# Linear attention and GeGLU on one core: denominators of all heads on column tiles, spread over the heads' rows by DMA

## The chip, the cores and the metric

The kernel runs on one core of a Trainium2 chip. The metric is the device time of one execution in microseconds (us), as the median of three runs. Five engines work side by side, each through its own instructions in order: PE (TensorE, matmuls; its weight loads are listed as PEld), DVE (VectorE), ACT (ScalarE), POOL (GpSimd) and SP (SyncE, which issues most of the DMA transfers). They wait for one another by semaphores.

## What is computed

A layer norm, a linear attention with 32 heads of 18 columns and a gated MLP, all on the same normalised input of 2048 tokens with 576 features, summed with the input:

```python
def _A_ref(x, wqkv, wo):                       # S = 2048, D = 576, H = 32, Dh = 18
    qkv = (x @ wqkv).reshape(B, S, 3, H, Dh).transpose(2, 0, 3, 1, 4)
    q, k, v = qkv[0], qkv[1], qkv[2]
    phi = lambda t: jnp.where(t > 0, t + 1, jnp.exp(t)) + 1e-6
    pq, pk = phi(q), phi(k)
    kv = jnp.einsum("bhsd,bhse->bhde", pk, v)
    z = jnp.einsum("bhsd->bhd", pk)
    num = jnp.einsum("bhqd,bhde->bhqe", pq, kv)
    den = jnp.einsum("bhqd,bhd->bhq", pq, z)[..., None] + 1e-6
    return (num / den).transpose(0, 2, 1, 3).reshape(B, S, D) @ wo

def _B_ref(x, w_gate, w_up, w_down):           # F = 4608
    return (_gelu(x @ w_gate) * (x @ w_up)) @ w_down

xn = _layernorm(x)
return x + _A_ref(xn, A_wqkv, A_wo) + _B_ref(xn, B_w_gate, B_w_up, B_w_down)
```

The denominator `den` is one number for each token and head. It divides 18 columns of the numerator, so it may as well divide the 18 rows of that head in the transposed `pq`.

## The kernel before

**Data.** `xnT` is the normalised input, transposed, features on the partitions. `pqT` is the transposed phi(q) in five chunks of heads: four of 7 heads (126 rows) and one of 4 heads (72 rows), each with 2048 tokens. Tokens are worked on in four groups of 512 (`sc` = 0 to 3). A unit of Q is one chunk of one group, 20 in all.

**Front** (to about 71 us). The layer norm, K, phi(K), the matrix G of phi(K) and the input, and most Q units run in an order written out by due times (`STEPS`, `Q_STEPS`, lines 530 to 583). What follows is written out as program order (lines 600 to 640): the rest of G, its copies to SBUF (`g_copy`), Q unit 12, the last rows of G (`g_last`), the column sums of phi(K) (`z_sums`, which uses four column tiles of 32), their copies (`z_copies`), Q unit 13, then `z_stage` and `kv_stage`. `z_stage` makes `zrep`: for each chunk a matrix in which every row of a head has that head's z, repeated for the head's 18 columns and masked elsewhere. A matmul with it gives the denominator already repeated over the head's rows. The last six Q units run as three pairs on row tiles (`q_pair`, `_Unit`): two units share the array, each on 64 of its rows, take nine slots instead of ten, and change places on the PSUM banks half way (`p1`, `p2`). For the change of places an empty instruction on another engine (the relay: SP for these pairs, POOL in the gate/up blocks after the first) waits for `p1` and releases `p2`.

**Gate/up stage** of each token group (`gu_pair`): 18 blocks of two units, each unit 18 row-tiled matmuls. ACT makes the gelu of one bank, DVE multiplies the other bank into `hT`. A block's weights (`wg`, `wu`, `wr`, four transfers) go to one of four buffers; they are issued on SP at the start of the block three earlier (`load_gu(blk + NWBUF - 1, i)`). In the first group, blocks 2 to 13 also issue one slice each of the down weights `wd_sb`.

**Denominators.** In the first group, blocks 2 to 4 carry three row-tiled pairs of denominator matmuls (`den_pair`, lines 498 and 687 to 699). The others (`den_mm`, line 495) run at the head of the half tiles of the down stage before. DVE copies each result to SBUF and adds the epsilon (`den_evac`), then inverts it in pieces of 128 columns (`den_norm`, line 519), and POOL multiplies `pqT` by it (line 522).

**Down stage** of each token group (`down_tile`): four tiles of 128 tokens in two halves of 288 columns; each half is 36 matmuls of `hT` with `wd_sb` (line 724) and 5 of `pqT` with `m_sb` (line 729). `m_sb` is made once from kv and wo (`m_stage`). DVE adds the input and SP writes the tile out. `hooks` lists what goes ahead of a half's matmuls.

Of the kernel before, what the change touches and what calls it, by code (L numbers as in the profile page):

```python
# [9 lines left out]
ALU = mybir.AluOpType  # L10
# [5 lines left out]
P = 128  # L16
HP = 64
# [22 lines left out]
TD = 4  # L40
XW = 640
PKW = 580


class _Ring:
# [11 lines left out]
def kernel(  # L57
# [68 lines left out]
    make_identity(nc, ident[:])  # L126
    eps_ln = const.tile([P, 1], F32, name="eps_ln")
    nc.vector.memset(eps_ln[:], EPS_LN)
    eps_att = const.tile([P, 1], F32, name="eps_att")
    nc.vector.memset(eps_att[:], EPS_ATT)  # L130

    def spin(count):

# [6 lines left out]
    pqT = persist.tile([P, NCH, S], BF16, name="pqT")  # L140
    wo2 = persist.tile([P, NCH, D], BF16, name="wo2")
    m_sb = persist.tile([P, NCH, D], BF16, name="m_sb")
    zrep = persist.tile([P, NCH, CR], BF16, name="zrep")
    kvT = persist.tile([P, NCH, CR], BF16, name="kvT")

    nc.vector.memset(pqT[HP:P, NCH - 1, 0:2 * SC], 0.0)
    nc.vector.memset(zrep[HP:P, NCH - 1, :], 0.0)

    def load_wo():
        nc.sync.dma_start(wo2[:CR, 0:4, :], A_wo[0:4 * CR, :].rearrange("(c p) j -> p c j", p=CR))  # L150
# [49 lines left out]
    nc.gpsimd.memset(g_sb[0:HP, 4, HALF:D], 0.0)  # L200
    nc.gpsimd.memset(g_sb[HP:P, 4, 0:HALF], 0.0)

    ZQ = 32
    z_ones = const.tile([P, ZQ], BF16, name="z_ones")
    nc.gpsimd.memset(z_ones[:], 1.0)
    z_sb = apool.tile([P, D], BF16, name="z_sb")
    nc.gpsimd.memset(z_sb[:], 0.0)
    zsel = const.tile([P, CR], BF16, name="zsel")
    nc.gpsimd.memset(zsel[:], 0.0)
    for g in range(P // ZQ):  # L210
        nc.gpsimd.memset(zsel[g * ZQ:g * ZQ + 1, :], 1.0)
# [109 lines left out]
    def z_sums(bank):  # L321
        for n in range(NS):
            for g in range(4):
                p0 = PK0[g // 2] + (g % 2) * DQ
                nc.tensor.matmul(
                    ps_all[g * ZQ:(g + 1) * ZQ, bank, 0:DQ], lhsT=z_ones[:], rhs=pk[:, n, p0:p0 + DQ],
                    start=(n == 0), stop=(n == NS - 1), skip_group_check=True,
                )
# [52 lines left out]
    def q_unit(i):  # L381
        sc, c = divmod(i, NCH)
        rows = DH * HCH[c]
        q0 = DH * HOFF[c]
        ps = ps_all[:rows, q_banks.next(), :]
        for kt in range(KT):
            nc.tensor.matmul(  # L387
                ps, lhsT=wqkv_sb[:, kt, q0:q0 + rows], rhs=xnT[:, kt, sc * SC:(sc + 1) * SC],
                start=(kt == 0), stop=(kt == KT - 1),
            )  # L390
        q_out[i] = ps
# [57 lines left out]
    def mask_pair(dst, b4, b1):  # L449

        nc.vector.tensor_tensor(
            out=dst[:CR, 0:4, :], in0=ps_all[:CR, b4, 0:4 * CR].rearrange("p (c d) -> p c d", c=4),
            in1=bmask[:CR, :].unsqueeze(1).to_broadcast([CR, 4, CR]), op=ALU.mult,
        )
        r4 = DH * HCH[4]
        nc.vector.tensor_tensor(
            out=dst[:r4, 4, :r4], in0=ps_all[:r4, b1, 0:r4], in1=bmask[:r4, :r4], op=ALU.mult,
        )

    def chunk_out(c, b4, b1):  # L460
        rows = DH * HCH[c]
        return ps_all[:rows, b4, c * CR:c * CR + rows] if c < 4 else ps_all[:rows, b1, 0:rows]

    def z_stage(b4, b1):
        for c in range(NCH):
            rows = DH * HCH[c]
            nc.tensor.matmul(
                chunk_out(c, b4, b1), lhsT=z_sb[:, c * CR:c * CR + rows], rhs=zsel[:, :rows],
                start=(c in (0, 4)), stop=True, skip_group_check=True,
            )  # L470
        mask_pair(zrep, b4, b1)

    def kv_stage(b4, b1):
        for kt in range(KT):
# [6 lines left out]
                )  # L481
        mask_pair(kvT, b4, b1)

    den_sb = {}

    def den_evac(sc, c, ps):
        rows = DH * HCH[c]
        d = dwork.tile([P, SC], F32, name="den_sb", tag="den_sb", bufs=6)
        nc.vector.tensor_scalar_add(out=d[:rows, :], in0=ps, scalar1=EPS_ATT)
        den_sb[sc, c] = d  # L490

    def den_mm(sc, c, bank):
        rows = DH * HCH[c]
        ps = ps_all[:rows, bank, :]
        nc.tensor.matmul(ps, lhsT=zrep[:rows, c, :rows], rhs=pqT[:rows, c, sc * SC:(sc + 1) * SC], start=True, stop=True)  # L495
        den_evac(sc, c, ps)

    def den_pair(items, outs):

        rows = DH * HCH[items[0][1]]  # L500

        def part(r):

            return slice(r.start, min(r.stop, P if rows <= P - HP + 8 else rows))

        return _Unit(
            outs,
            lambda i, r, kt: zrep[part(r), items[i][1], :rows],
            lambda i, r, kt: pqT[part(r), items[i][1], items[i][0] * SC:(items[i][0] + 1) * SC],
            nc.sync, first=(0,), then=(0,),  # L510
        )

    def den_norm(sc, c, q, pieces):
        w = SC // pieces
        rows = DH * HCH[c]
        d = den_sb[sc, c][:rows, q * w:(q + 1) * w]
        cols = slice(sc * SC + q * w, sc * SC + (q + 1) * w)
        for h in range(0, w, P):
            nc.vector.reciprocal(out=d[:, h:h + P], in_=d[:, h:h + P])  # L519

        def scale():
            nc.gpsimd.tensor_tensor(out=pqT[:rows, c, cols], in0=pqT[:rows, c, cols], in1=d, op=ALU.mult)  # L522
        return scale

# [84 lines left out]
    g_copy(1, (3, 288), [(ALL, 3, 0, 288, 288, nc.scalar), (ALL, 2, 0, 0, 288, nc.vector)])  # L611
    for _, step, n in todo[tail:]:
        step(n)
    q_unit(12)
    for step in (q_exp1, q_min, q_max):
        step(12)
    g_last(0)
    z_sums(1)
    g_copy(3, (6, 288), [(ALL, 6, 0, 288, 288, nc.scalar), (ALL, 5, 0, 0, 288, nc.vector)])
    g_copy(4, (0, 288), [(HI, 0, 0, 288, 288, nc.scalar), (LO, 0, 0, 0, 288, nc.vector)])  # L620
    z_copies(1)
    q_unit(13)
    z_stage(2, 3)
    kv_stage(6, 5)
    for step in (q_exp1, q_min, q_max):
        step(13)


    q_banks = _Ring(list(range(6)))
    prev = None  # L630
    for units in [[15, 16], [17, 18], [14, 19], None]:
        if units:
            u = q_pair(units)
            u.p1()
        if prev:
            prev[1].p2()
            for step in (q_exp1, q_min, q_max):
                for i in prev[0]:
                    step(i)
        prev = (units, u)  # L640
    scales = []
    den_jobs = [(0, c, q, 2) for c in range(NCH) for q in range(2)]

    asmall_cm.__exit__(None, None, None)
    awork_cm.__exit__(None, None, None)
# [9 lines left out]
            nc.sync.dma_start(wd_sb[:, f0:f0 + WDS, :], wd_view[:, f0:f0 + WDS, :])  # L655
            wd_loaded[0] += WDS


    DEN_FROM = 2
    DEN_PAIRS = [[(0, 0), (0, 1)], [(0, 2), (0, 3)], [(0, 4), (1, 4)]]  # L660

    def gu_pair(sc, k):
        cs = slice(sc * SC, (sc + 1) * SC)
        blk = sc * (NF // GUB) + k
        wg, wu, wr = gu_blocks.pop(blk)
        units = []
        for i in range(GUB):
            b = [banks.next(), banks.next()]
            fcol = slice(i * P, (i + 1) * P)

            def lhs(a, rows, kt, fcol=fcol):
                if kt == 4:
                    return wr[rows, fcol]
                return (wg, wu)[a][rows, kt, fcol]

            u = _Unit([ps_all[:, b[0], :], ps_all[:, b[1], :]], lhs, lambda a, rows, kt: xnT[rows, kt, cs],
                      nc.sync if blk == 0 else nc.gpsimd)
            if blk > 0:
                load_gu(blk + NWBUF - 1, i)
            u.p1()  # L680
            units.append((b, u))
        if sc == 0 and k == 1:
            load_wo()
        elif sc == 0 and k >= 2:
            load_wd_slice()
        den = None
        if sc == 0 and 0 <= k - DEN_FROM < len(DEN_PAIRS):
            items = DEN_PAIRS[k - DEN_FROM]
            den = den_pair(items, [ps_all[:DH * HCH[c], banks.next(), :] for _, c in items])
            den.p1()  # L690
        for i, (b, u) in enumerate(units):
            u.p2()
            gl = fwork.tile([P, SC], F32, name="gl")
            nc.scalar.activation(out=gl[:], in_=ps_all[:, b[0], :], func=ACT.Gelu_apprx_tanh)  # L694
            nc.vector.tensor_tensor(out=hT[:, GUB * k + i, :], in0=ps_all[:, b[1], :], in1=gl[:], op=ALU.mult)  # L695
        if den:
            den.p2()
            for (dsc, c), ps in zip(items, den.outs):
                den_evac(dsc, c, ps)

    def m_stage(c, acc_bank):
        rows = DH * HCH[c]
# [8 lines left out]
    def down_tile(sc, j, hooks):  # L711
# [23 lines left out]
        if not last:  # L735
            nc.sync.dma_start(out_view[:, n, :], res[:])

    for sc in range(NSC):
        for k in range(NF // GUB):
            gu_pair(sc, k)  # L740
            if scales:
                scales.pop(0)()
            if den_jobs and k > DEN_FROM:
                scales.append(den_norm(*den_jobs.pop(0)))
        while wd_loaded[0] < NF:
            load_wd_slice()

        hooks = [{6 * c_: (lambda b, c_=c_: m_stage(c_, b)) for c_ in range(NCH)} if sc == 0 else {}]
        if sc + 1 < NSC:
            for c_ in range(NCH):  # L750
                def dn(b, c=c_, nsc=sc + 1):
                    if (nsc, c) not in den_sb:
                        den_mm(nsc, c, (b + 2) % 8)
                    den_norm(nsc, c, 0, 1)()
                hooks.append({0: dn})
        for j in range(TPC):
            down_tile(sc, j, hooks)

# [29 lines left out]
```

## Time and profile before

| what | value |
|---|---|
| median of three runs | 524.05 us (523.87 to 524.52) |
| the profiled execution | 523.49 us |
| its span, first to last instruction | 521.8 us |
| DVE reciprocals (line 519), all forms | 80, 68.3 us |
| DVE copies of denominators (line 489), 126 rows | 16, 680 ns each |
| POOL scaling of `pqT` (line 522), all forms | 25, 24.1 us |
| bytes read from HBM | 52.94 MB |
| DMA packets of SP's queue | 105706, 38.8% of 16 engines' span |

A group's line has the source line, the engine, the operation, what it writes and reads, the shapes, the count, and then the busy time in us and the mean of one in ns. The last column is the time that the engine stood just ahead of such instructions, and for what. Ends of matmuls are modelled, and two row tiles run at once, so the busy times of the PE groups add up to more than the span; how fast PE goes is read from the chain of waits, which has start, duration and count. In the table by stretch, DMA share is the part of the 16 DMA engines' time that packets took.

### The profile page before, as it was taken

Reading aid. Unit: us, or ns where it says so; the run is one execution under the profiler, and the core shown is the slowest. Engines: PE = TensorE matmul, PEld = TensorE weight load, DVE = VectorE, ACT = ScalarE, POOL = GpSimd, SP = SyncE. Lnnn points to the kernel's source line nnn. Section 1 sums busy time; section 2 is a strip of 40 time slices with the busy share of each in tenths; the row PEclk is TensorE's granted clock in tenths of the full one; section 3 lists DMA queues with packets and bytes.
Section 4 is the critical chain, followed back from the end, with each engine's and each line's share of the span. In section 5 each row is a group of like instructions: output and inputs, shape, how many; then the busy total and the mean of one; then the engine's idle time right before and its main releaser. Section 6 shows DMA issues by size and latency. Waiting matters only on the chain.

```text
span 521.8 us, 10779 instructions
## 1 busy us (share of the span) xinstructions
PE 516.3 (99%) x4562; PEld 313.8 (60%) x4562; DVE 251.2 (48%) x438; ACT 143.8 (28%) x296; POOL 36.4 (7%) x62
## 2 busy tenths in 40 slices
PE   8999999999999999999999999999999999999997
PEld 7777755555587754444577644444777544445775
DVE  7996565876358323433388033333584233333100
ACT  6899442322320013323200032332000123322000
POOL 3011000211001100000012000000011000000000
PEclk9999999999999999999999999999999999999999
DMA  8434509898500045455300155555000355540000
GB/s 267 75 62 122 155 27 264 238 287 258 162 13 13 11 126 158 142 159 157 92 13 13 43 163 152 158 147 157 26 25 13 105 159 158 142 133 1 13 13 23
DMA packets 106362, 57.96 MB, mean 111 GB/s; under 512 B 13386, under 2 KB 105802, under 8 KB 106314
## 3 DMA queue, kind: packets, MB, share of 16 engines
q1 hardware_dynamic: 105706, 56.62, 38.8%
q8 instruction: 35, 0.57, 0.5%
q10 hardware_dynamic: 608, 0.66, 0.4%
q14 instruction: 13, 0.11, 0.1%
HBM read 52.94 MB, written 2.36 MB: 106 GB/s over the span
## 4 chain that ended last, share of the span: by engine, by line
PE 96%; ACT 1%; DMA 1%; DVE 1%; issue 0%; ACTq 0%
PE ps_all L358 55%; PE ps_all L724 27%; PE ps_all L729 4%; PE ps_all L259 3%; PE ps_all L303 3%; PE ps_all L387 3%; DMA wqkv_sb<-in_A_wqkv_dram 1%; PE ps_all L495 1%; PE ps_all L477 0%; PE ps_all L706 0%; ACT xnT L248 0%; ACT L116 0%; DVE g_sb L597 0%; ACT phi_e L279 0%; ACT z_sb L335 0%; DVE pqT L447 0%
## 5 line engine op out<-in xcount | busy, mean ns | idle before, releaser
L358 PE MATMUL ps_all<-xnT,wg 64*128 64x512 bf16 x1152 | 272.7, 376 | 0.0
L358 PE MATMUL ps_all<-xnT,wu 64*128 64x512 bf16 x1152 | 271.8, 376 | 0.0
L695 DVE TENSOR_TENSOR hT<-ps_all,gl 128x512 bf16<-128x512 f32 x144 | 99.4, 691 | 162.0 <-ACT gl L694 161.3
L694 ACT ACTIVATE gl<-ps_all 128x512 f32<-128x512 f32 x144 | 86.0, 597 | 314.4 <-PE ps_all L358 295.0
L358 PEld LDWEIGHTS <-wu 64*128 64x128 bf16 x1152 | 108.3, 94 | 66.2
L358 PEld LDWEIGHTS <-wg 64*128 64x128 bf16 x1152 | 108.3, 94 | 66.0
L724 PE MATMUL ps_all<-wd_sb,hT 128*128 128x288 bf16 x1152 | 147.0, 286 | 0.0
L724 PEld LDWEIGHTS <-hT 128*128 128x128 bf16 x1152 | 112.3, 98 | 30.7 <-issue 1.3
L519 DVE RECIPROCAL den_sb<-den_sb 126x128 f32<-126x128 f32 (+1 forms) x80 | 68.3, 910 | 0.5
L732 DVE TENSOR_TENSOR res<-ps_all,x_sb 128x288 bf16<-128x288 f32 x32 | 14.6, 457 | 88.0 <-PE ps_all L729 88.0
L358 PE MATMUL ps_all<-xnT,wr 64*128 64x512 bf16 x288 | 55.2, 376 | 0.0
L522 POOL TENSOR_TENSOR pqT<-pqT,den_sb 126x512 bf16<-126x512 bf16 (+3 forms) x25 | 24.1, 965 | 317.0 <-DVE den_sb L519 282.4
L729 PE MATMUL ps_all<-m_sb,pqT 126*128 126x288 bf16 (+1 forms) x160 | 24.9, 286 | 0.0
L358 PEld LDWEIGHTS <-wr 64*128 64x128 bf16 x288 | 14.5, 94 | 16.8 <-issue 0.7
L259 PE MATMUL ps_all<-wqkv_sb,xnT 128*128 128x288 bf16 x160 | 22.5, 286 | 0.6 <-DMA wqkv_sb<-in_A_wqkv_dram 0.5
L259 PEld LDWEIGHTS <-xnT 128*128 128x128 bf16 x160 | 15.3, 98 | 6.7 <-issue 0.8
L303 PE MATMUL ps_all<-hT,xn 128*128 128x288 bf16 (+4 forms) x144 | 18.2, 273 | 0.0
L729 PEld LDWEIGHTS <-pqT 126*128 126x128 bf16 (+1 forms) x160 | 15.5, 97 | 4.1
L387 PE MATMUL ps_all<-xnT,wqkv_sb 128*126 128x512 bf16 (+1 forms) x70 | 17.4, 379 | 0.0
L303 PEld LDWEIGHTS <-xn 128*128 128x128 bf16 x144 | 13.9, 98 | 3.3
L287 DVE SCALAR_TENSOR_TENSOR hT<-ps_all,phi_e 128x288 bf16<-128x288 f32 x32 | 13.2, 449 | 4.4 <-ACT phi_e L283 3.8
L279 ACT ACTIVATE phi_e<-ps_all 128x288 f32<-128x288 f32 x32 | 12.9, 409 | 3.4 <-PE ps_all L259 1.9
(78 smaller groups left out, 184.7 us busy)
## 6 DMA issues: line engine op xcount, KB each, us to landing
wg<-in_B_w_gate_dram SPq DMA_DIRECT2D x72, 256.0 KB, 2.8
wu<-in_B_w_up_dram SPq DMA_DIRECT2D x72, 256.0 KB, 3.5
wd_sb<-in_B_w_down_dram SPq DMA_DIRECT2D x12, 432.0 KB, 4.5
wr<-in_B_w_gate_dram SPq DMA_DIRECT2D x72, 32.0 KB, 2.6
wr<-in_B_w_up_dram SPq DMA_DIRECT2D x72, 32.0 KB, 3.0
out_dram<-res SPq DMA_DIRECT2D x15, 144.0 KB, 1.8
x_sb<-in_A_x_dram SPq DMA_DIRECT2D x3, 576.0 KB, 7.4
wqkv_sb<-in_A_wqkv_dram SPq DMA_DIRECT2D x2, 576.0 KB
```

The lines of the kernel that those rows point to most:

```text
L259: nc.tensor.matmul(ps_all[:, k_bank(n, hf), :HALF], lhsT=xnT[:, kt, n * P:(n + 1) * P], rhs=wqkv_sb[:, kt, D + hf * HALF:D + (hf + 1) * HALF],
L287: nc.vector.scalar_tensor_tensor(out=out_, in0=ps, scalar=0.0, in1=e, op0=ALU.max, op1=ALU.add)
L303: nc.tensor.matmul(ps_all[:, b, col:col + w], lhsT=xn[:, n, kt * P:(kt + 1) * P], rhs=pk[:, n, p0:p0 + w], start=(n == 0 and col == 0), st ...
L358: return nc.tensor.matmul(self.outs[i], lhsT=self.lhs(i, rows, kt), rhs=self.rhs(i, rows, kt), start=start, stop=stop, skip_group_check=True,)
L387: nc.tensor.matmul(ps, lhsT=wqkv_sb[:, kt, q0:q0 + rows], rhs=xnT[:, kt, sc * SC:(sc + 1) * SC], start=(kt == 0), stop=(kt == KT - 1),)
L519: nc.vector.reciprocal(out=d[:, h:h + P], in_=d[:, h:h + P])
L522: nc.gpsimd.tensor_tensor(out=pqT[:rows, c, cols], in0=pqT[:rows, c, cols], in1=d, op=ALU.mult)
L694: nc.scalar.activation(out=gl[:], in_=ps_all[:, b[0], :], func=ACT.Gelu_apprx_tanh)
L695: nc.vector.tensor_tensor(out=hT[:, GUB * k + i, :], in0=ps_all[:, b[1], :], in1=gl[:], op=ALU.mult)
L724: nc.tensor.matmul(acc, lhsT=hT[:, f, j * P:(j + 1) * P], rhs=wd_sb[:, f, hs], start=(f == 0), stop=False,)
L729: nc.tensor.matmul(acc, lhsT=pqT[:rows, c, ts_], rhs=m_sb[:rows, c, hs], start=False, stop=(c == NCH - 1),)
L732: nc.vector.tensor_tensor(out=res[:, hs], in0=acc, in1=x_sb[:, n, hs], op=ALU.add)
```

## The change

The denominators are now computed once for each head, not once for each of its rows. `z_stage` makes `zden`, which has one column for each head: 7 columns for each of the first four chunks, and the last chunk's 4 heads in columns 8 to 11. `den_mm` computes all heads of one token group in one PSUM bank: chunk g (0 to 3) on the column tile of 32 g, giving rows 32 g to 32 g + 6; the last chunk's tokens are cut into four quarters, and quarter g lands in rows 32 g + 8 to 32 g + 11. One DVE instruction copies the bank and adds the epsilon; four reciprocals of 128 x 128 invert it. SP then issues transfers inside SBUF that read each head's row 18 times and write it to the 18 rows of the head in `den_rep` (`den_spread`): one transfer for each of the first four chunks, four for the last. POOL multiplies `pqT` by `den_rep` as before, in the same pieces.

The denominators of groups 0 and 1 are computed at the end of the front, those of groups 2 and 3 in the down stages of groups 0 and 1. Group 0 is inverted in blocks 2 to 5 of its gate/up stage, spread in blocks 6 (three chunks) and 7 (two), and scaled in blocks 8 to 17. Group 1 is inverted in blocks 6 to 9; groups 1 to 3 are spread and scaled in the down stage of the group before.

Q units 12 and 13 leave their places as full-array units and run as a fourth row-tiled pair, ahead of the other three. `z_sums` goes ahead of `g_last`, and `z_copies` ahead of the copy of G's last rows.

```diff
-    def z_stage(b4, b1):
+    def z_stage(b):
         for c in range(NCH):
             rows = DH * HCH[c]
             nc.tensor.matmul(
-                chunk_out(c, b4, b1), lhsT=z_sb[:, c * CR:c * CR + rows], rhs=zsel[:, :rows],
-                start=(c in (0, 4)), stop=True, skip_group_check=True,
+                ps_all[:rows, b, c * ZQ:(c + 1) * ZQ], lhsT=z_sb[:, c * CR:c * CR + rows], rhs=zsel[:],
+                start=(c == 0), stop=True, skip_group_check=True,
             )
-        mask_pair(zrep, b4, b1)
+        heads = bmask[:].rearrange("p (h e) -> p h e", e=DH)[:, :, 0]
...
+    def den_mm(sc, bank):
+        for g in range(4):
+            nc.tensor.matmul(
+                ps_all[g * ZQ:(g + 1) * ZQ, bank, :], lhsT=zden[:CR, g, :], rhs=pqT[:CR, g, sc * SC:(sc + 1) * SC],
+                start=True, stop=False, skip_group_check=True,
+            )
+        r4 = DH * HCH[4]
+        for g in range(4):
+            t0 = sc * SC + g * TQ
+            nc.tensor.matmul(
+                ps_all[g * ZQ:(g + 1) * ZQ, bank, g * TQ:(g + 1) * TQ], lhsT=zden[:r4, 4, :],
+                rhs=pqT[:r4, 4, t0:t0 + TQ], start=False, stop=True, skip_group_check=True,
+            )
+
+    def den_evac(sc, bank):
+        d = dwork.tile([P, SC], F32, name="den_sb", tag="den_sb", bufs=2)
+        nc.vector.tensor_scalar_add(out=d[:], in0=ps_all[:, bank, :], scalar1=EPS_ATT)
+        den_sb[sc] = d
+
+    def den_recip(sc, q):
+        d = den_sb[sc][:, q * P:(q + 1) * P]
+        nc.vector.reciprocal(out=d, in_=d)
+
+    def den_spread(sc, c):
+        d = den_sb[sc]
+        if sc not in den_rep:
+            den_rep[sc] = dwork.tile([P, NCH, SC], F32, name="den_rep", tag="den_rep", bufs=1)
+        to = den_rep[sc]
+        nh = HCH[c]
+        rows = DH * nh
+        if c < 4:
+            parts = [(c * ZQ, 0, SC)]
+        else:
+            parts = [(g * ZQ + Z4, g * TQ, TQ) for g in range(4)]
+        for p0, t0, w in parts:
+            nc.sync.dma_start(
+                to[:rows, c, t0:t0 + w],
+                d[p0:p0 + nh, t0:t0 + w].unsqueeze(1).to_broadcast([nh, DH, w]),
+            )
...
-    q_unit(12)
-    for step in (q_exp1, q_min, q_max):
-        step(12)
+    z_sums(1)
     g_last(0)
-    z_sums(1)
     g_copy(3, (6, 288), [(ALL, 6, 0, 288, 288, nc.scalar), (ALL, 5, 0, 0, 288, nc.vector)])
+    z_copies(1)
     g_copy(4, (0, 288), [(HI, 0, 0, 288, 288, nc.scalar), (LO, 0, 0, 0, 288, nc.vector)])
-    z_copies(1)
-    q_unit(13)
-    z_stage(2, 3)
-    kv_stage(6, 5)
-    for step in (q_exp1, q_min, q_max):
-        step(13)
+    z_stage(2)
+    kv_stage(4, 5)
+    for sc, bank in ((0, 3), (1, 2)):
+        den_mm(sc, bank)
+        den_evac(sc, bank)
...
-    for units in [[15, 16], [17, 18], [14, 19], None]:
+    for units in [[12, 13], [15, 16], [17, 18], [14, 19], None]:
...
+    den_jobs = {k: [] for k in range(NF // GUB)}
+    for q in range(4):
+        den_jobs[2 + q].append(lambda q=q: den_recip(0, q))
+        den_jobs[6 + q].append(lambda q=q: den_recip(1, q))
+    for c in range(NCH):
+        den_jobs[6 + c // 3].append(lambda c=c: den_spread(0, c))
+        for q in range(2):
+            den_jobs[8 + 2 * c + q].append(lambda c=c, q=q: den_scale(0, c, q, 2))
...
+        if sc + 1 < NSC:
+            for c in range(NCH):
+                jobs[1].append(lambda b, c=c, n=sc + 1: den_spread(n, c))
+                jobs[3 + c].append(lambda b, c=c, n=sc + 1: den_scale(n, c))
+        if sc + 2 < NSC:
+            jobs[2].append(lambda b, n=sc + 2: (den_mm(n, (b + 2) % 8), den_evac(n, (b + 2) % 8)))
+            for q in range(4):
+                jobs[3 + q].append(lambda b, q=q, n=sc + 2: den_recip(n, q))
```

More of the change, by code (lines that the diff above doesn't have):

```diff
@@ L42 @@
 PKW = 580
+ZQ = 32
+Z4 = 8
 class _Ring:
@@ L128 @@
     nc.vector.memset(eps_ln[:], EPS_LN)
-    eps_att = const.tile([P, 1], F32, name="eps_att")
-    nc.vector.memset(eps_att[:], EPS_ATT)
     def spin(count):
@@ L142 @@
     m_sb = persist.tile([P, NCH, D], BF16, name="m_sb")
-    zrep = persist.tile([P, NCH, CR], BF16, name="zrep")
+    zden = persist.tile([P, NCH, ZQ], BF16, name="zden")
     kvT = persist.tile([P, NCH, CR], BF16, name="kvT")
-    nc.vector.memset(pqT[HP:P, NCH - 1, 0:2 * SC], 0.0)
-    nc.vector.memset(zrep[HP:P, NCH - 1, :], 0.0)
+    nc.gpsimd.memset(zden[:], 0.0)
     def load_wo():
@@ L201 @@
     nc.gpsimd.memset(g_sb[HP:P, 4, 0:HALF], 0.0)
-    ZQ = 32
     z_ones = const.tile([P, ZQ], BF16, name="z_ones")
@@ L207 @@
     nc.gpsimd.memset(z_sb[:], 0.0)
-    zsel = const.tile([P, CR], BF16, name="zsel")
+    zsel = const.tile([P, ZQ], BF16, name="zsel")
     nc.gpsimd.memset(zsel[:], 0.0)
@@ L467, in z_stage @@
             nc.tensor.matmul(
-                chunk_out(c, b4, b1), lhsT=z_sb[:, c * CR:c * CR + rows], rhs=zsel[:, :rows],
-                start=(c in (0, 4)), stop=True, skip_group_check=True,
-            )
-        mask_pair(zrep, b4, b1)
+                ps_all[:rows, b, c * ZQ:(c + 1) * ZQ], lhsT=z_sb[:, c * CR:c * CR + rows], rhs=zsel[:],
+                start=(c == 0), stop=True, skip_group_check=True,
+            )
+        heads = bmask[:].rearrange("p (h e) -> p h e", e=DH)[:, :, 0]
+        nc.vector.tensor_tensor(
+            out=zden[:CR, 0:4, 0:7], in0=ps_all[:CR, b, 0:4 * ZQ].rearrange("p (c h) -> p c h", c=4)[:, :, 0:7],
+            in1=heads[:CR].unsqueeze(1).to_broadcast([CR, 4, 7]), op=ALU.mult,
+        )
+        r4 = DH * HCH[4]
+        nc.vector.tensor_tensor(
+            out=zden[:r4, 4, Z4:Z4 + HCH[4]], in0=ps_all[:r4, b, 4 * ZQ:4 * ZQ + HCH[4]],
+            in1=heads[:r4, 0:HCH[4]], op=ALU.mult,
+        )
     def kv_stage(b4, b1):
@@ L482, in kv_stage @@
         mask_pair(kvT, b4, b1)
-    den_sb = {}
-    def den_evac(sc, c, ps):
-        rows = DH * HCH[c]
[L488 to L510, printed above, removed]
-        )
[L513 to L523, printed above, removed]
+    den_sb, den_rep = {}, {}
@@ new lines @@
+    TQ = SC // 4
+    def den_mm(sc, bank):
[4 more added lines that the diff above has]
+            )
+        r4 = DH * HCH[4]
+        for g in range(4):
[3 more added lines that the diff above has]
+                rhs=pqT[:r4, 4, t0:t0 + TQ], start=False, stop=True, skip_group_check=True,
+            )
@@ new lines, in den_evac @@
+    def den_evac(sc, bank):
[20 more added lines that the diff above has]
+                d[p0:p0 + nh, t0:t0 + w].unsqueeze(1).to_broadcast([nh, DH, w]),
+            )
@@ L528, with den_scale @@
+    def den_scale(sc, c, q=0, pieces=1):
+        rows = DH * HCH[c]
+        w = SC // pieces
+        cols = slice(sc * SC + q * w, sc * SC + (q + 1) * w)
+        nc.gpsimd.tensor_tensor(
+            out=pqT[:rows, c, cols], in0=pqT[:rows, c, cols], in1=den_rep[sc][:rows, c, q * w:(q + 1) * w], op=ALU.mult,
+        )
     TILE = 2.94
@@ L613 @@
         step(n)
-    q_unit(12)
-    for step in (q_exp1, q_min, q_max):
-        step(12)
+    z_sums(1)
     g_last(0)
-    z_sums(1)
     g_copy(3, (6, 288), [(ALL, 6, 0, 288, 288, nc.scalar), (ALL, 5, 0, 0, 288, nc.vector)])
+    z_copies(1)
     g_copy(4, (0, 288), [(HI, 0, 0, 288, 288, nc.scalar), (LO, 0, 0, 0, 288, nc.vector)])
-    z_copies(1)
-    q_unit(13)
-    z_stage(2, 3)
-    kv_stage(6, 5)
-    for step in (q_exp1, q_min, q_max):
-        step(13)
-    q_banks = _Ring(list(range(6)))
+    z_stage(2)
[3 more added lines that the diff above has]
+        den_evac(sc, bank)
+    q_banks = _Ring([6, 7, 0, 1, 2, 3, 4, 5])
     prev = None
-    for units in [[15, 16], [17, 18], [14, 19], None]:
+    for units in [[12, 13], [15, 16], [17, 18], [14, 19], None]:
         if units:
@@ L640 @@
         prev = (units, u)
-    scales = []
-    den_jobs = [(0, c, q, 2) for c in range(NCH) for q in range(2)]
     asmall_cm.__exit__(None, None, None)
@@ L656, in load_wd_slice @@
             wd_loaded[0] += WDS
-    DEN_FROM = 2
-    DEN_PAIRS = [[(0, 0), (0, 1)], [(0, 2), (0, 3)], [(0, 4), (1, 4)]]
     def gu_pair(sc, k):
@@ L685, in gu_pair @@
             load_wd_slice()
[L686 to L690, printed above, removed]
         for i, (b, u) in enumerate(units):
@@ L695, in gu_pair @@
             nc.vector.tensor_tensor(out=hT[:, GUB * k + i, :], in0=ps_all[:, b[1], :], in1=gl[:], op=ALU.mult)
[L696 to L699, printed above, removed]
     def m_stage(c, acc_bank):
@@ L740 @@
             gu_pair(sc, k)
[L741 to L744, printed above, removed]
+            for job in den_jobs.pop(k, ()):
+                job()
         while wd_loaded[0] < NF:
             load_wd_slice()
-        hooks = [{6 * c_: (lambda b, c_=c_: m_stage(c_, b)) for c_ in range(NCH)} if sc == 0 else {}]
+        hooks = [{} for _ in range(2 * TPC)]
+        if sc == 0:
+            hooks[0] = {6 * c_: (lambda b, c_=c_: m_stage(c_, b)) for c_ in range(NCH)}
+        jobs = [[] for _ in range(2 * TPC)]
         if sc + 1 < NSC:
[L750 to L755, printed above, removed]
+            for c in range(NCH):
[5 more added lines that the diff above has]
+                jobs[3 + q].append(lambda b, q=q, n=sc + 2: den_recip(n, q))
+        for todo, js in zip(hooks, jobs):
+            if js:
+                todo[0] = lambda b, js=js: [job(b) for job in js]
         for j in range(TPC):
```

## The prediction

> **What bounds the kernel now.** I read the page's busy times first, then the chain of waits. PE is busy for 99% of the span and the chain is PE work nearly from end to end, so only PE time that goes away, or PE idle time that appears, moves the end. Page and chain (start us, us, what, instructions):
>
> ```profile
> PE 516.3 (99%) x4562; PEld 313.8 (60%) x4562; DVE 251.2 (48%) x438; ACT 143.8 (28%) x296; POOL 36.4 (7%) x62
> ...
> 57.75 1.09 PE ps_all L387 x5
> ...
> 64.18 1.43 PE ps_all L477 x25
> 65.61 77.21 PE ps_all L358 x714
> ...
> 149.23 0.22 PE ps_all L495
> 149.45 4.41 PE ps_all L724 x36
> ...
> 185.30 70.03 PE ps_all L358 x648
> ```
>
> A gate/up stage without denominators takes 70.03 us for 324 slots of two row-tiled matmuls: 0.2161 us a slot, 3.89 us for a block of 18. A denominator matmul in the down stage costs 0.22 us (14 of them).
>
> Then the groups by form, for the rows of the denominators and of the column-tiled sums:
>
> ```profile
> L519 DVE RECIPROCAL den_sb<-den_sb 126x128 f32<-126x128 f32 x64 | 54.7, 911 | 0.4
> L495 PE MATMUL ps_all<-pqT,zrep 126*126 126x512 bf16 x12 | 4.6, 379 | 0.0
> L325 PE MATMUL ps_all<-hT,z_ones 128*32 128x144 bf16 x64 | 1.2, 226 | 0.0
> ```
>
> Last, because the change adds transfers to SP's queue, busy time by stretch (PE, PEld, DVE, ACT, POOL, clock, DMA share, GB/s) and SP's issues by time (start us, us) in the first gate/up stage:
>
> ```profile
> 103.50:107.40 3.90, 3.90 (x40) 2.07 (x36) 3.05 (x4) 1.21 (x3) 0.61 (x2) 1.00 1.05 318
> 111.20:115.10 3.90, 3.90 (x40) 2.08 (x38) 3.05 (x4) 1.21 (x3) 0.68 (x2) 1.00 0.96 273
> 134.30:138.20 3.90, 3.90 (x40) 2.08 (x38) 1.38 (x2) 1.21 (x3) 0.00 (x0) 1.00 0.54 154
> ...
> 107.88 0.37 SPq L173 DMA_DIRECT2D wg<-in_B_w_gate_dram  x1
> 108.30 0.52 SPq L174 DMA_DIRECT2D wr<-in_B_w_gate_dram  x1
> 108.86 0.59 SPq L176 DMA_DIRECT2D wu<-in_B_w_up_dram  x1
> 109.49 0.51 SPq L177 DMA_DIRECT2D wr<-in_B_w_up_dram  x1
> 110.04 0.59 SPq L655 DMA_DIRECT2D wd_sb<-in_B_w_down_dram  x1
> 111.77 0.37 SPq L173 DMA_DIRECT2D wg<-in_B_w_gate_dram  x1
> ```
>
> While `wd_sb` is loaded (blocks 2 to 13) the DMA engines are 85 to 105% taken; afterwards 54%. A block's weights are issued three blocks ahead, 3 x 3.89 = 11.7 us before PE needs them. The last is issued 1.6 us into the block and lands 3.4 us later (median there), so the slack is 11.7 - 1.6 - 0.5 - 3.4, about 6.2 us.
>
> [...]
>
> **The change part by part.**
>
> *Down stages.* 14 matmuls of L495 go: 14 x 0.217 = 3.04 us. Two `den_mm` come: each has four 32-column matmuls of 512 columns on four column tiles, then four of 128. L325 shows four such tiles side by side: 64 matmuls of 144 columns in a row would take 64 x 0.061 = 3.9 us (0.061 is half of 4.41/36), and they take 1.1. So `den_mm` is 0.216 + 0.054 = 0.27 us; four in a row would be 1.08, the upper bound. Net -2.50.
>
> *First gate/up stage.* Three row-tiled pairs of two slots go: 6 x 0.2161 = -1.30 us (the chain agrees: 77.21 - 70.03 is 33 slots, 27 for Q and 6 for these).
>
> *Front, 57.75 to the gate/up start.* Before, PE takes 7.86 us to 65.61, then three Q pairs of 1.945 us, to 71.45. In it lie two full-array Q units (1.09 each) and a gap near 63 us in which z waits for the serial chain of `z_copies`. Now: z_sums 1.12, g_last 2.02, a 32-column z stage some 0.2, kv 1.43, two `den_mm` 0.54, four pairs 7.78: 70.84. The Q fillers are gone, but `z_sums` now stands ahead of `g_last`, whose 2.0 us cover the 1.4 us chain of copies; the copy of G's last rows (1.2 us) lies under kv's first 20 matmuls (1.14). The masks of `zden` lie under kv's last five. I take -0.5; with the cover gone it is up to +1.
>
> *Allowance* for changing tile shapes around four `den_mm`: +0.2 (bounds 0 and 0.8). PE work sums to -2.50 - 1.30 - 0.5 + 0.2 = -4.1 us.
>
> *DVE.* Reciprocals fall from 80 to 16 (68.3 to 14.6 us), evacuations from 20 to 4. Nothing on the path: PE never waited for DVE. Three memsets leave DVE and one joins POOL at the start, under the weight load that ends at 7.22. POOL's 25 scalings stay.
>
> *The spreads* are what is not free. Chunk c's 7 rows sit on partitions 32c to 32c+6, each read 18 times at 2 KB. [...]
>
> For stages 1 to 3 they run in a down stage of 40 us, DMA nearly idle: hidden; four outputs queue behind, with three `res` buffers. For stage 0 they are issued in blocks 6 and 7, in front of the weights of blocks 10 and 11. [...] From block 6's start: weights and `wd_sb` issued by 2.8, served by about 6.2; [...] block 10's weights land at 24.6, needed at 15.5: PE stands 9 us. [...] block 11's weights at 39.3, needed at 28.5: 10.8 more. In all 19.8 us[...]. Block 12's land at 43, just in time. [...]
>
> *POOL's new wait*: `den_scale` waits for a spread's landing, and behind it queue the relay nops for the second halves of the next block's units. The first scaling could start at 12.5 and end at 13.3; the relay is needed at 13.8. No cost taken.
>
> **Sum.** -4.1 + 19.8 + 1.7 = +17.4 us. The profiled execution is 523.49 (span 521.8 and 1.7 around it), giving 540.9; the median of runs is 0.56 above it: 541.4. I write 541.
>
> **Rivals.**
>
> *A: no port limit (0.25).* [...] Then only the PE sum is left: 524.05 - 4.1 = 519.9, faster. For it: the change's PE work is plainly less and the DMAs lie two blocks ahead of the scaling. Against: the share of 0.96 leaves no room for eight transfers from a few partitions. [...]
>
> *B: the port carries twice that (0.15).* [...] -4.1 + 6 = +2, perhaps 1.7 more: 526.
>
> *C: the column tiles don't overlap or the front stands (0.05).* The PE gain falls from 4.1 to about 0.5, with no DMA cost: 523.5.
>
> **How the numbers follow.** Forecast 0.55, A 0.25, B 0.15, C 0.05. The forecast's own range is 535 to 549: the port 15% faster and no cold clock, or 25% slower. The range for 8 in 10 reaches to A: 519.3 to 547. Measurement can tell 0.2%, about 1 us. Faster: A and a little of B and C, 0.29. Same: 0.04. Slower: 0.67.
>
> **What would show it.** Right: PE idle for some 9 and 11 us at the starts of blocks 10 and 11 (near 110 to 135 us), released by a weight transfer; spreads landing 5 to 20 us after issue; a clock below 1.00 once after it; no L495 in the down stages and 5.03 us per half. Wrong: spreads landing in 3 us, the first gate/up stage at 70 us without a gap. A loss in the down stages, at the front or on DVE would mean that I mispriced something else.

## The result and the profile after

The changed kernel takes 541.93 us (median of 4 runs, 541.51 to 542.53) against 524.25 for the kernel before in the same comparison. The ratio is 1.034, with a 95% interval of 1.032 to 1.036: slower. The profiled execution took 542.53 us with a span of 540.7, 18.9 us more than the span before.

The page of the changed kernel, PE busy and granted clock in 40 slices of 13.5 us:

```profile
PE   8999999924999999999999999999999999999997
...
PEclk9999999977899999999999999999999999999999
```

The damage is in one place, slices 8 to 10 (counted from 0), from about 108 to 149 us. The waits of PE say for what it stood (total us, times, longest):

```profile
PE ps_all L356 <- DMA wr<-in_B_w_gate_dram: 15.7, 2, 9.6
PE ps_all L135 <- POOL ident masks.py:199: 1.4, 1, 1.4
PE ps_all L356 <- DMA wr<-in_B_w_up_dram: 1.2, 2, 1.0
```

16.9 us of standing for gate/up weights, where the kernel before had none. The chain of waits shows the way there (start us, us, what):

```profile
63.60 45.92 PE ps_all L356 x424
109.52 0.32 SPq L172
109.84 0.05 issue
109.89 3.67 SPq L173
113.57 0.04 issue
113.61 3.96 SPq L175
...
131.53 2.92 DMA wr<-in_B_w_up_dram
134.45 0.05 issue
134.50 29.32 PE ps_all L356 x251
```

The chain leaves PE near the end of block 9, runs through SP's queue for 22 us, and comes back with the last weight of block 11. The first slot of the first block is at 63.60 + 36 x 0.2161 = 71.38 us, so block 11 was due at 71.38 + 11 x 3.89 = 114.2; after a single matmul at 132.9 it gets going at 134.50, 20.3 us late. The 16.9 us of standing are most of that; the rest is block 10, which PE ran largely at half clock (0.50 until 124.8 us). The seven blocks from there take 29.32 us instead of 27.2: 2.1 more, because PE comes back with half a clock (0.50). Stretches of the same execution show it (PE, PEld, DVE, ACT, POOL, clock, DMA share, GB/s):

```profile
110.20:114.00 3.80, 0.17 (x2) 0.00 (x0) 2.22 (x3) 0.60 (x1) 0.00 (x0) 1.00 0.49 99
114.00:118.00 4.00, 0.00 (x0) 0.00 (x0) 0.00 (x0) 0.00 (x0) 0.00 (x0) 0.58 0.25 35
...
134.50:138.40 3.90, 3.90 (x20) 1.42 (x22) 0.00 (x0) 0.00 (x0) 0.00 (x0) 0.50 1.08 319
138.40:142.30 3.90, 3.90 (x40) 1.71 (x38) 1.38 (x2) 1.19 (x2) 0.67 (x1) 0.99 1.07 306
```

From 134.50 PE counts as busy, yet starts 20 matmuls where it starts 40 in the next stretch of the same length. And while it stands, the DMA engines are far from full: 99 and 35 GB/s. The bytes were not too many; something held them. SP's issues by time (start us, us, transfer, count) say what stood in front:

```profile
98.51 0.59 SPq L670 DMA_DIRECT2D wd_sb<-in_B_w_down_dram  x1
99.20 6.62 SPq L532 DMA_DIRECT2D den_rep<-den_sb  x3
105.92 3.93 SPq L172 DMA_DIRECT2D wg<-in_B_w_gate_dram  x1
109.89 3.67 SPq L173 DMA_DIRECT2D wr<-in_B_w_gate_dram  x1
113.61 3.96 SPq L175 DMA_DIRECT2D wu<-in_B_w_up_dram  x1
117.62 0.52 SPq L176 DMA_DIRECT2D wr<-in_B_w_up_dram  x1
118.18 0.59 SPq L670 DMA_DIRECT2D wd_sb<-in_B_w_down_dram  x1
118.81 9.18 SPq L532 DMA_DIRECT2D den_rep<-den_sb  x5
```

Three spreads take SP 6.6 us, and the first three weight transfers behind them 3.7 to 4.0 us each, where most issues of a weight took 0.4 to 0.6.

In the down stage, where little else runs on the DMA engines (share 0.04 and 13 GB/s in the kernel before, from 143 to 185 us), one can see the rate of a spread. DMA share and GB/s of the changed kernel from 160 to 200 us, in 40 slices of 1 us:

```profile
DMA  1757233434443334433322222222214400000400
GB/s 35 225 156 210 31 45 45 49 47 49 55 88 55 57 53 49 64 53 51 49 39 25 25 25 27 25 45 55 50 33 146 164 9 0 0 0 0 148 0 0
```

About 50 GB/s with three to four tenths of the 16 engines until 180 us, then 25 with two tenths until 186. The slower stretch isn't yet that of the small transfers: the fourth large spread lands only near 188, where the scaling that waits for it starts (188.36, shown below). Suppose that of a spread's seven rows the first four are read one after another, and the other three one after another beside them: an assumption of the author's that no trace of before showed. The three have a quarter less to do and are done first, so two sets of rows at some 25 GB/s, and then one, would fit both rates. Seven rows that are each slow by themselves would end together. That is a first sign, but an argument only; the experiments had to tell the theories apart.

### The profile page after: what moved, and what is told of

It is laid out like the page before. It is cut to its first block, busy times and chain, and to the rows that moved or that the text cites. A ratio compares the mean times of both kernels' runs of the same rounds, so it can differ in the third digit from the quotient of the medians.

```text
span 540.7 us, 10764 instructions
## 1 busy us (share of the span) xinstructions
PE 518.1 (96%) x4576; PEld 307.7 (57%) x4576; DVE 187.3 (35%) x355; ACT 143.8 (27%) x296; POOL 36.2 (7%) x63
## 4 chain that ended last, share of the span: by engine, by line
PE 93%; SPq 4%; DMA 2%; ACT 1%; DVE 0%; issue 0%
PE ps_all L356 53%; PE ps_all L727 26%; PE ps_all L732 4%; PE ps_all L257 3%; PE ps_all L301 3%; PE ps_all L385 2%; SPq L532 2%; DMA wqkv_sb<-in_A_wqkv_dram 1%; SPq L173 1%; SPq L175 1%; DMA wr<-in_B_w_up_dram 1%; PE ps_all L310 0%; PE ps_all L484 0%; SPq L172 0%; PE ps_all L709 0%; PE ps_all L498 0%
## 5 line engine op out<-in xcount | busy, mean ns | idle before, releaser
L356 PE MATMUL ps_all<-xnT,wg 64*128 64x512 bf16 x1152 | 275.7, 379 | 0.0
L356 PE MATMUL ps_all<-xnT,wr 64*128 64x512 bf16 x288 | 60.2, 383 | 16.9 <-DMA wr<-in_B_w_gate_dram 15.7
L541 POOL TENSOR_TENSOR pqT<-pqT,den_rep 126x512 bf16<-126x512 bf16 (+3 forms) x25 | 24.1, 966 | 332.8 <-DMA den_rep<-den_sb 284.4
L356 PEld LDWEIGHTS <-wr 64*128 64x128 bf16 x288 | 15.7, 95 | 36.4 <-DMA wr<-in_B_w_gate_dram 16.7
L301 PEld LDWEIGHTS <-xn 128*128 128x128 bf16 x144 | 13.9, 98 | 3.3
L517 DVE RECIPROCAL den_sb<-den_sb 128x128 f32<-128x128 f32 x16 | 15.1, 943 | 0.0
L385 PE MATMUL ps_all<-xnT,wqkv_sb 128*126 128x512 bf16 (+1 forms) x60 | 14.9, 378 | 0.0
L285 DVE SCALAR_TENSOR_TENSOR hT<-ps_all,phi_e 128x288 bf16<-128x288 f32 x32 | 13.2, 450 | 4.4 <-ACT phi_e L281 3.6
```

What stands on the lines that cost most here:

```text
L285: nc.vector.scalar_tensor_tensor(out=out_, in0=ps, scalar=0.0, in1=e, op0=ALU.max, op1=ALU.add)
L301: nc.tensor.matmul(ps_all[:, b, col:col + w], lhsT=xn[:, n, kt * P:(kt + 1) * P], rhs=pk[:, n, p0:p0 + w], start=(n == 0 and col == 0), st ...
L356: return nc.tensor.matmul(self.outs[i], lhsT=self.lhs(i, rows, kt), rhs=self.rhs(i, rows, kt), start=start, stop=stop, skip_group_check=True,)
L385: nc.tensor.matmul(ps, lhsT=wqkv_sb[:, kt, q0:q0 + rows], rhs=xnT[:, kt, sc * SC:(sc + 1) * SC], start=(kt == 0), stop=(kt == KT - 1),)
L517: nc.vector.reciprocal(out=d, in_=d)
```

## The experiments

Three theories were open. **Ports**: source rows that lie in the same four partitions are read one after another, as if through one port; "port" is only the author's name for that assumption. **Few engines**: a transfer that keeps only some of the 16 DMA engines busy (two to four tenths above) is slow wherever its rows lie. **Crowding of the queue**: eight more transfers in two blocks, with their issues and semaphores, hold up the weights. The first two runs leave everything as it is and only move the heads' rows apart. That takes a step in three places:

```diff
-            out=zden[:CR, 0:4, 0:7], ...
+            out=zden[:CR, 0:4, 0:6 * HS + 1:HS], ...
-            out=zden[:r4, 4, Z4:Z4 + HCH[4]], ...
+            out=zden[:r4, 4, Z4:Z4 + 3 * Z4S + 1:Z4S], ...
-                d[p0:p0 + nh, t0:t0 + w].unsqueeze(1).to_broadcast([nh, DH, w]),
+                d[p0:p0 + (nh - 1) * step + 1:step, t0:t0 + w].unsqueeze(1).to_broadcast([nh, DH, w]),
```

**Rows four partitions apart** (`HS` = 4, `Z4` = 2, `Z4S` = 8).

> The only change to the changed kernel: each head's row lies four partitions from the next (0, 4, ... 24 of each 32; the last chunk's heads at 2, 10, 18, 26)[...]. [...] Port theory: [...] PE doesn't stand in the first gate/up stage, and what is left is the PE gain read from the trace of the changed kernel, 3.5 us: 520.7 us (519.5 to 522). Rival, few engines[...]: no difference, 541 to 543. Rival, number of transfers on SP[...]: no difference, 541 to 543.

Measured: 522.65 us (521.61 to 525.32 in 20 runs), ratio to before 0.9988 (0.9977 to 0.9999). Without any spread in the first stage the kernel takes 520.42 us (two runs below), 21.5 less than the changed kernel; 19.3 of these are gone here, with not one transfer less. Both rivals fall as the main cause. It is 2 us slower than the port theory said, outside its range, and not steady; more on that below.

**Rows two partitions apart** (`HS` = 2, `Z4` = 16, `Z4S` = 2).

> As the run before, with rows two partitions apart (0, 2, ... 12; the last chunk's at 16, 18, 20, 22)[...]. Port theory: [...] PE stands some 6 us and pays 2 us of cold clock: 528.7 us (524 to 531), and scalings in the down stages start 2.7 to 3 us apart where the changed kernel has 5.2 to 6.0. Few engines or number of transfers: 541 to 543, scalings 5 to 6 us apart.

Measured: 528.52 us (527.42 to 529.78), ratio 1.0084 (1.0068 to 1.0101). The dose works. POOL's scalings in the down stage start as each spread lands, where the line names the DMA as the releaser; first the changed kernel, then rows two apart, then four apart (start us, us, and in brackets the idle time ahead of it and its releaser):

```profile
171.48 1.16 POOL L541 TENSOR_TENSOR pqT<-pqT,den_rep 126x512 bf16<-126x512 bf16 x1 [8.44 <-DMA den_rep<-den_sb]
177.19 1.16 POOL L541 TENSOR_TENSOR pqT<-pqT,den_rep 126x512 bf16<-126x512 bf16 x1 [4.55 <-DMA den_rep<-den_sb]
183.13 1.16 POOL L541 TENSOR_TENSOR pqT<-pqT,den_rep 126x512 bf16<-126x512 bf16 x1 [4.78 <-DMA den_rep<-den_sb]
188.36 1.16 POOL L541 TENSOR_TENSOR pqT<-pqT,den_rep 126x512 bf16<-126x512 bf16 x1 [4.06 <-DMA den_rep<-den_sb]
```

```profile
154.13 1.16 POOL L543 TENSOR_TENSOR pqT<-pqT,den_rep 126x512 bf16<-126x512 bf16 x1 [5.11 <-PE ps_all L711]
157.25 1.16 POOL L543 TENSOR_TENSOR pqT<-pqT,den_rep 126x512 bf16<-126x512 bf16 x1 [1.96 <-DMA den_rep<-den_sb]
...
162.82 1.16 POOL L543 TENSOR_TENSOR pqT<-pqT,den_rep 126x512 bf16<-126x512 bf16 x1 [1.58 <-DMA den_rep<-den_sb]
```

```profile
146.24 1.16 POOL L543 TENSOR_TENSOR pqT<-pqT,den_rep 126x512 bf16<-126x512 bf16 x1 [3.54 <-DMA den_rep<-den_sb]
...
150.88 1.17 POOL L543 TENSOR_TENSOR pqT<-pqT,den_rep 126x512 bf16<-126x512 bf16 x1 [0.26 <-DMA den_rep<-den_sb]
```

Each spread reads the same 36.9 KB from every row. The table takes a third of the time from the first scaling to the fourth; with rows two apart the first scaling was released by PE, so there it is half the time from the second to the fourth:

| rows within the same four partitions | time of one spread | bytes of these rows / time |
|---|---|---|
| 4 (one apart) | (188.36 - 171.48) / 3 = 5.63 us | 147.5 KB: 26.2 GB/s |
| 2 (two apart) | (162.82 - 157.25) / 2 = 2.79 us | 73.7 KB: 26.4 GB/s |
| 1 (four apart) | (150.88 - 146.24) / 3 = 1.55 us | 36.9 KB: 23.8 GB/s |

The time goes with the spacing: 5.63, 2.79 and 1.55 us for rows one, two and four apart. The bytes of the rows within four partitions move at 26.2, 26.4 and 23.8 GB/s. What sets the 1.55 us, these runs don't show. SP's issue goes with the spacing too: the median over all 32 spreads of a run, large and small, is 3.58 us with rows one apart, 1.80 with two and 0.84 with four.

**Without the spreads of group 0.** Their two jobs are left out:

```diff
-        den_jobs[6 + c // 3].append(lambda c=c: den_spread(0, c))
-        for q in range(2):
-            den_jobs[8 + 2 * c + q].append(lambda c=c, q=q: den_scale(0, c, q, 2))
```

> The changed kernel without the spreads and the scalings of token group 0, so the attention of the first 512 tokens isn't divided. Port theory, and every theory in which the transfers of the first stage are the whole loss: 520.7 us (519.5 to 522), no stand of PE. If the loss came from anything else (the new front, the column tiles, the later spreads), some of it stays: above 523.

Measured: 520.42 us (520.22 to 520.99), ratio 0.9939 (0.9924 to 0.9953), no stand of PE in the first gate/up stage. The rest of the change is a gain of 3.3 us, and the whole loss, 21.5 us, comes with the transfers of the first stage and the scalings behind them, which went too.

**The transfers alone, in the kernel before.** Eight transfers of the same kind, with no other part of the change:

```diff
+    def spread7(c):
+        nh, rows = HCH[c], DH * HCH[c]
...
+        parts = [(c * 32, 0, 1024)] if c < 4 else [(g * 32 + 8, g * 256, 256) for g in range(4)]
+        for p0, t0, w in parts:
+            nc.sync.dma_start(
+                to[:rows, t0:t0 + w], x_flat[p0:p0 + nh, t0:t0 + w].unsqueeze(1).to_broadcast([nh, DH, w]),
+            )
...
             gu_pair(sc, k)
+            if sc == 0 and k in (6, 7):
+                for c in range(3) if k == 6 else (3, 4):
+                    spread7(c)
```

> The kernel before, with eight transfers of the same shapes, bytes and places in SP's queue put into blocks 6 and 7 of its first gate/up stage; they read rows of the input (7 or 4 rows next to each other, each 18 times) and write into SBUF that is not yet in use. If the transfers alone make the loss: the 21 us between the changed kernel and e3_no_spread0 on top of before, 545 us (543 to 547). If the loss needs something else of the change: less than 540.

Measured: 544.63 us (543.17 to 545.99), ratio 1.0393 (1.0377 to 1.041). Taking them out of the changed kernel gives 21.5 us back (21.0 when each of the two is taken against the kernel before as measured beside it, 524.25 and 523.7), putting them into the other costs 20.8. So the transfers are needed for the loss, and without scalings and without the rest of the change they are enough for it.

**The same, with the rows far apart.** If what matters were only that the rows are neighbours, rows 16 apart would be free. The author expected that they aren't.

```diff
-        parts = [(c * 32, 0, 1024)] if c < 4 else [(g * 32 + 8, g * 256, 256) for g in range(4)]
+        parts = [(c, 0, 1024)] if c < 4 else [(g + 8, g * 256, 256) for g in range(4)]
+        step = 16 if c < 4 else 32
...
-                ... x_flat[p0:p0 + nh, t0:t0 + w].unsqueeze(1) ...
+                ... x_flat[p0:p0 + (nh - 1) * step + 1:step, t0:t0 + w].unsqueeze(1) ...
```

> As e6_before_with_spreads, but the rows of a transfer lie 16 partitions apart (0, 16, ... 96) and those of the small ones 32 apart. [...] some 8 us on top of before, 532 us (529 to 534). Rival, only neighbouring rows (within the same four partitions) get in each other's way: one row each, no more than 2 us on top of before, 524 to 526.

Measured: 533.06 us (532.03 to 533.68), ratio 1.0171 (1.0158 to 1.0184): 9.3 us. So rows 16 apart cost less than neighbours (20.8) but aren't free; they cost about what rows two apart cost in the changed kernel (8.1 us over the kernel without the spreads of group 0). Which of the far rows get in each other's way, no run shows.

**Crowded rows, one transfer a block.** The changed kernel with its rows as they are, but the eight transfers in blocks 6 to 13 (`den_spread` also gets an argument that picks one of the last chunk's four; not shown):

```diff
-        den_jobs[6 + c // 3].append(lambda c=c: den_spread(0, c))
+        for i in range(1 if c < 4 else 4):
+            den_jobs[6 + c + i].append(lambda c=c, i=i: den_spread(0, c, i))
```

> The changed kernel, rows next to each other as there[...], but the transfers of group 0 one in each of blocks 6 to 13. Port theory: [...] 536 to 541 us, in more and shorter stands. Rival, crowding in time (eight transfers in two blocks, with their waits on the semaphores, are what hurts): 520 to 523.

Measured: 536.11 us (534.85 to 537.44), ratio 1.0231 (1.0214 to 1.0248). In the profiled execution PE stands 9.6 us in seven pieces of up to 3 us. Spreading them in time saves 5.8 of the 21.5 us. The transfers have to go somewhere, and while the down weights are loaded the DMA engines of the kernel before are 85 to 105% taken.

**Rows four apart, one transfer a block** (the same edit on the first run).

> As e1_one_per_port, and the eight transfers of group 0 are issued one in each of blocks 6 to 13, where they were three in block 6 and five in block 7. In e1_one_per_port PE stood 1.3 us ahead of block 11, whose last weight transfer waited for the spread eight transfers before it. Port theory with the slack: [...] no weight is late, and the time is that without the spreads of group 0: 520.4 us (519.8 to 521.5). If what e1_one_per_port has over e3_no_spread0 came from the later spreads or the scalings, it stays at 522 to 523.

Measured: 522.03 us (520.25 to 523.87 in 12 runs), ratio 0.9967 (0.9955 to 0.9979). A miss by 1.6 us, and a scatter of 3.6. In the profiled execution, one of the quicker ones (520.93), PE waits 0.2 us for a weight. The slower executions were not profiled, so that late weights made them slow is likely, not shown. The chain shows how little was left, and where it went: through a weight transfer that took 7.5 us, and then the last weight of a block, 5.9.

```profile
63.79 44.80 PE ps_all L358 x413
108.59 7.53 DMA wg<-in_B_w_gate_dram
116.12 0.02 issue
116.14 0.50 SPq L177
116.64 0.04 issue
116.68 5.90 DMA wr<-in_B_w_up_dram
122.58 0.05 issue
122.63 19.60 PE ps_all L358 x179
```

**After the down weights** (again with rows four apart). So the transfers went where the table of stretches of before showed room (DMA share 0.54), behind the last slice of `wd_sb`:

```diff
-        den_jobs[6 + c // 3].append(lambda c=c: den_spread(0, c))
+        den_jobs[14 + c // 3].append(lambda c=c: den_spread(0, c))
         for q in range(2):
-            den_jobs[8 + 2 * c + q].append(lambda c=c, q=q: den_scale(0, c, q, 2))
+            den_jobs[15 + c // 2].append(lambda c=c, q=q: den_scale(0, c, q, 2))
```

> As e1_one_per_port[...], with the spreads of group 0 in blocks 14 and 15, after the last slice of the down weights, and its scalings in blocks 15 to 17. There the DMA engines were 54% taken in the kernel before, so a weight has its whole slack again. Port theory with the slack: no late weight in any execution, 520.4 us (519.8 to 521.2), and a scatter as small as that of e3_no_spread0 (under 1 us between executions) where e4_one_a_block had 3.6. If the rest of e4_one_a_block over e3_no_spread0 (1.6 us) is the work of the later spreads or the scalings, 522.

Measured: 520.69 us (520.36 to 521.42), ratio 0.9941 (0.9927 to 0.9955), a scatter of 1.1. No weight is late in the profiled execution, and time and steadiness are close to those of the kernel without these transfers (520.42, a scatter of 0.8). So the later spreads and the scalings are not what the run before had lost. The waits of PE hold one surprise:

```profile
PE ps_all L358 <- POOLq L367: 1.3, 1, 1.3
```

This is the relay: POOL stood 3.56 us at a scaling of chunk 3 whose spread had not landed, and the empty instruction that lets the second half of a gate/up unit start was queued behind it.

**Scalings later.** `15 + c // 2` becomes `[15, 16, 16, 17, 17][c]`. So only chunks 1 and 3 move, each by one block.

> As e8_after_wd, with the scalings of chunks 1 to 4 one or two blocks later (blocks 16, 16, 17, 17). In e8_after_wd the weights were on time, but PE stood 1.3 us in block 17 for POOL's relay, which was queued behind a scaling of chunk 3 that waited for its spread. If that is the rest, it goes: 519.4 us (518.8 to 520.2) and no wait of PE in the first gate/up stage. If the relay is late behind scalings in any case, or the rest is work, 520.4 to 521.4.

Measured: 520.33 us (519.71 to 520.56), ratio 0.9936 (0.9922 to 0.9949). PE waits for nothing after its warm-up at the start (its only wait is the 1.4 us for `ident`), so the relay's wait is gone. The time can't be told from that of the run before: the intervals overlap. It is 0.9 us above the expectation, so what the wait of 1.3 us was worth stays open. With 3.3 us less than the kernel before, this run and the one before it are the quickest complete versions here.

## Why the prediction came out right

**The stand of PE.** Said: 19.8 us. Measured: block 11 comes 20.3 us late. The pieces differ: 9.8 us ahead of block 10 (9 was said), and 7.1 instead of 10.8 ahead of block 11, because block 10 got going 1.4 us later than said (120.75) and then ran largely at half clock. The end was set by the arrival of block 11's weights, and it was sized well: 134.5 against 134.0 us. How long the spreads take was the author's estimate, made without a trace that showed one. That the closeness of their rows makes them slow is shown by the runs with rows two and four apart (5.63 us for a large spread as it is, 2.79 and 1.55 in these). In the first down stage the four large ones at 5.63 us, with 3.7 us for the last chunk's four together (from 188.36, the start of the fourth scaling, to 192.05, that of the fifth), make 26.2 us. What sets the time of the small ones, no run tried.

**How the weights came to be late** was right in effect, and in part different in place. The prediction had them land late behind the spreads. In the trace most of the delay lies ahead of that, in the issues: three spreads keep SP for 6.6 us and the three weights behind them for 3.7 to 4.0 us each. Block 10's last weight is issued at 117.6 us, where block 7, at whose start it was due, began at 98.6; it lands 3 us later. A part comes after the issue: the weight that ends the first stand, a `wr`, was issued by 113.6 us and let PE go at 119.96, 6.4 us later, where no `wr` took more than 5.2 before. What made SP's issues so long was not shown. That the size of the stand came out all the same fits a stand whose end depends on when the spreads are through, wherever the weights wait. SP's waits for the landing of earlier transfers were not tried alone. In the run with rows four apart one shows: a spread issued at 106.23 us lands at 112.36, SP issues block 11's last weight at 112.38, and PE stands 1.2 us ahead of that block.

**The cold clock.** Said: 1.7 us, once, the author's estimate; in the trace of before the clock is 1.00 throughout. Measured: 2.1, once. The clock is 0.50 for about 4.0 us from PE's return (134.50 to 138.5), and was so for 4.1 after the first stand (120.75 to 124.8). That first cold start doesn't count at the end: PE stands again for block 11's weights from 126.8 us on.

**The PE work.** Said: -4.1 us. Measured in the trace: -3.4, which the runs without late weights confirm (3.2 to 3.3 us quicker than before). Two terms were mis-sized. The first is the changes of tile shape, for which 0.2 us was allowed in all. A `den_mm` itself was priced well: in the front, where two follow each other, the second takes 0.22 + 0.06 us, and 0.27 was said. The chain of the changed kernel prices one in the down stage:

```profile
170.23 4.41 PE ps_all L727 x36
174.64 0.62 PE ps_all L732 x5
175.26 0.33 PE ps_all L498 x4
175.59 0.06 PE ps_all L505 x4
175.64 4.52 PE ps_all L727 x36
```

0.33 + 0.06 (0.38 from 175.26 to 175.64), and the 36 matmuls behind it take 4.52 instead of 4.41: 0.49 in all. So a change of tile shape costs 0.11 us on the way in (0.33 against 0.22) and 0.11 on the way out. The kernel before shows the second, too, at the first half tile after a row-tiled gate/up stage:

```profile
255.34 4.52 PE ps_all L724 x36
```

Two such `den_mm` in the down stages give 3.04 - 0.98 = 2.06 where 2.50 was said. The second is the front, which was to gain 0.5 and gained 0.07: `g_last`, `z_stage` and the two `den_mm` took 0.08, 0.17 and 0.12 more than said, and this execution's weights landed 0.14 later. The first gate/up stage gave its 1.30.

The sum: 20.3 + 2.1 - 3.4 = 19.0 against 18.9 measured, and 17.4 said. Errors of some half a microsecond in three terms all went the same way.

**The rivals.** A, that the spreads make no stand, is refuted by the changed kernel (16.9 us); even with rows four apart, at 1.55 us a spread, those as placed fall just short of free (1.2 us). B, half the time for a spread, was put at 526, and the run with rows two apart is that case, with 2.79 us: 528.5. C, column tiles in a row, is out: four matmuls of 512 columns take 0.33 us, not 0.86.

**POOL's new wait** cost nothing in the changed kernel: its first scaling started at 107.9, 13.2 us after block 6's start, and ended at 13.9, against 12.5 and 13.3 said; PE has no wait for POOL in that trace after the start. That the margin was thin was right as well: moved close to the spreads, it cost 1.3 us of PE.

## What to carry to other kernels

Before a DMA reads few SBUF rows many times, look at how far apart those rows lie, and not only at the bytes: with seven rows, a step of four partitions instead of one took 19.3 us off the changed kernel, with no transfer and no instruction more. A large step is not better by itself: in the kernel before, rows 16 apart still cost 9.3 us, where neighbours cost 20.8. Put such transfers into a stretch whose DMA share is low (0.54 here), and ask which loads are queued behind them on the issuing engine and how much slack those have. An engine that relays between halves of another engine's work shouldn't be made to wait for a transfer ahead of the relay (1.3 us of PE here).

## What was unexpected of the hardware

The issue of a transfer isn't a fixed price: SP spent 0.84, 1.80 or 3.58 us (medians over a run's 32 spreads) with rows four, two or one partition apart, and with one apart 3.7 to 4.0 on innocent weight transfers behind them. And in PE's first stand the DMA engines moved 99 and then 35 GB/s in all, where the kernel before moves 278 and 269 in the same stretches (110.2 to 114 and 114 to 118 us). With the same transfers from rows four apart PE stands 1.2 us in that stage instead of 16.9: it was the place of the rows that held up the whole queue.
